# Reordered bit moves, block transposes and block loads in an attention-plus-MLP kernel

## The chip, the cores and the metric

The kernel runs on one core of one Trainium2 chip. The metric is the device time of one execution in microseconds (us), the median of several.

In the profile, TensorE's matmuls are PE and its weight loads PEld, VectorE is DVE, ScalarE is ACT, GpSimd is POOL, and SPq is the queue of SyncE, which issues most of the DMAs.

## The reference, cut to what matters

```python
q_bits = (einsum('bhsd,dk->bhsk', q, proj) > 0)       # 6 hash bits of each query, same for k
mask   = q_bucket[:, :, :, None] == k_bucket[:, :, None, :]
scores = where(mask, q @ k.T / sqrt(64), -1e9)        # batch 4, 8 heads, 768 x 768
attn   = softmax(scores) @ v
x = attn.transpose(0, 2, 1, 3).reshape(3072, 512)
out = silu(x @ w_in) @ w_out                          # 512 -> 2048 -> 512
```

The heads go in 16 pairs. The hash bits are put into spare rows of the q and k tiles, so that one matmul gives the score and the bucket's match; exp of it goes to the product with v. When the four pairs of a batch element are done, its MLP runs beside the attention of the next.

## The kernel before

The program is a list of 288 steps (w). At each step TensorE does one score matmul group, one attention step (av) and, from the ninth head on, a part of an MLP. Everything else is planned to a step, which sets the order in which instructions are given to their engines, and nothing more: an engine runs its own list as soon as each instruction's semaphores allow.

```python
    # pool tag "m": three PSUM buffers for h_ps, bp_ps (bit projections), tp_ps, and the MLP's outputs
    def mm1(ci, grp):
        hp = ps.tile([P, f, n], F32, tag="m", name="h_ps", bufs=3)
        ...                                        # TensorE: 4 matmuls of 128x512
        nc.scalar.activation(out=th, in_=hp, func=AF.Tanh, scale=0.5)
        after.append(lambda: nc.vector.scalar_tensor_tensor(   # g, at the next step; frees h_ps
            out=g[...], in0=th, scalar=1.0, in1=hp, op0=ALU.add, op1=ALU.mult))

    def bits_unit(pairs, i, par):                  # for pairs up to 7: two bit moves on VectorE
        for n in range(2):
            ...
            if n == 1 and par == 1:
                nc.vector.tensor_scalar(out=dst, in0=bits[pairs][r, :], ...)
            else:
                nc.vector.tensor_copy(out=dst, in_=bits[pairs][r, :])

    def block_unit(p, n):                          # L246
        nc.vector.transpose(out=dst, in_=qk_sb[p, "qk"[n]])

    t_first(1, 0, nc.vector.tensor_copy)           # start: second head's q out of PSUM
    ...
    for Q in range(2, NQUAD):                      # pairs 2Q and 2Q+1
        w0 = (Q - 1) * QST                         # QST = 36 steps
        for i in range(4 if Q > 2 else 0):
            w1 = w0 + (5, 9, 11, 14)[i]
            plan(w1, lambda Q=Q, i=i: block_unit(2 * Q + i // 2, i % 2))
            ...
        plan(w0 + 20, lambda Q=Q: proj_unit(2 * Q, 2 * Q + 1))
        for i in range(4):
            plan(w0 + 20,
                 lambda Q=Q, i=i: bits_unit((2 * Q, 2 * Q + 1), i // 2, i % 2))
        for i in range(2):
            ...
            for j in range(2):
                plan(w0 + 18 + 9 * i + 2 * j, lambda p=2 * Q + i, j=j: v_unit(p, (j,)))   # GpSimd
            if Q + 1 < NQUAD:
                plan(w0 + (20 if Q == 3 else 8) + i, lambda p=2 * Q + 2 + i: load_blocks(p))
    # x_unit(p), a transposing DMA on SyncE's queue, is planned at 2*NU*(p+1) + 9, that is 99 for p = 4
```

## Time and profile before

| | before |
|---|---|
| time, median of 3 (range) | 307.0 us (306.68 to 307.44) |
| the profiled execution | 308.2 us, span of the core 306.4 us |
| TensorE busy | 299.8 us, 98% of the span |
| TensorE's waits for a PSUM buffer that g frees | 2.4 us in two places |
| VectorE, ScalarE, GpSimd busy | 59%, 69%, 42% |

The lines themselves are in the prediction below. In the lines by time, the columns are start in us, length in us, engine, line of the kernel, operation, output<-input, shape, count; brackets at the end give how long the engine sat idle before the instruction and what ended it.

### The profile page before, as it was taken

The page shows a single profiled execution, that of the slowest core. Times are in us where ns is not written, and L with a number is a line of the kernel's source. Part 1 is how long each engine was busy: PE and PEld are TensorE (multiplying, and loading weights), DVE is VectorE, ACT ScalarE, POOL GpSimd, SP SyncE. Part 2 cuts the span into 40 slices and gives each one's busy share as a digit, 9 for nine tenths or more (in the row PEclk, how much of TensorE's full clock was granted, in tenths as well). Part 3 has the DMA queues.
Part 4 walks back from the last instruction along what each step waited for, and adds up shares of the span by engine and source line. Part 5 has one row for each costly group of instructions (what it writes and reads, how often), then busy time and mean ns, then how long its engine had stood idle before and what let it go on. Part 6 is the DMA issues. An engine that isn't in the chain of part 4 may idle for free.

```text
span 306.4 us, 7166 instructions
## 1 busy us (share of the span) xinstructions
PE 299.8 (98%) x2710; PEld 174.8 (57%) x2710; DVE 181.8 (59%) x342; ACT 210.2 (69%) x391; POOL 128.9 (42%) x203
## 2 busy tenths in 40 slices
PE   8999999988999999999999999999999999999996
PEld 3675855544666555545565665545566664446653
DVE  5797977789559534854597325864453342664332
ACT  5887989987777686878876666778877731543200
POOL 7589999368514842765138431675111100000000
PEclk9999999999999999999999999999999999999999
DMA  7999797999939825774048434111022013001112
GB/s 201 243 263 208 139 134 115 184 247 169 167 91 174 153 65 158 125 135 127 9 92 131 89 64 148 52 41 33 2 60 62 0 37 94 34 2 68 36 60 76
DMA packets 102786, 32.87 MB, mean 107 GB/s; under 512 B 90656, under 2 KB 99808, under 8 KB 102752
## 3 DMA queue, kind: packets, MB, share of 16 engines
q1 hardware_dynamic: 98368, 28.22, 42.8%
q0 software_dynamic: 4224, 4.19, 9.2%
q8 instruction: 21, 0.34, 0.5%
q14 instruction: 13, 0.11, 0.1%
q10 hardware_dynamic: 160, 0.00, 0.0%
HBM read 27.27 MB, written 6.29 MB: 110 GB/s over the span
## 4 chain that ended last, share of the span: by engine, by line
PE 89%; DVE 4%; DMA 4%; ACT 1%; SPq 1%; issue 0%; POOL 0%; ACTq 0%; POOLq 0%
PE o_ps L455 26%; PE h_ps L423 24%; PE s_ps L333 18%; PE o_ps L365 12%; DMA k_blk<-in_k_dram 4%; PE bp_ps L279 3%; PE tp_ps L185 2%; DVE g L429 1%; PE o_ps L441 1%; PE warm_ps L125 1%; PE tp_ps L198 1%; DVE qka L310 1%; PE bp_ps L225 1%; ACT u L336 1%; SPq L92 1%; DVE qk L246 1%
## 5 line engine op out<-in xcount | busy, mean ns | idle before, releaser
L336 ACT ACTIVATE u<-s_ps 128x512 f16<-128x512 f32 x288 | 156.3, 605 | 40.3 <-PE s_ps L333 39.8
L429 DVE SCALAR_TENSOR_TENSOR g<-th,h_ps 128x512 f16<-128x512 f32 x96 | 65.1, 684 | 75.9 <-ACT th L427 75.9
L423 PE MATMUL h_ps<-xT,win 128*128 128x512 f16 (+1 forms) x512 | 97.4, 325 | 2.4 <-DVE g L429 2.4
L365 PEld LDWEIGHTS <-u 128*128 128x128 f16 x1152 | 67.5, 98 | 42.8 <-ACT u L336 11.2
L455 PE MATMUL o_ps<-wout,g 128*128 128x512 f16 x368 | 91.6, 379 | 0.0
L427 ACT ACTIVATE th<-h_ps 128x512 f32<-128x512 f32 x96 | 57.3, 597 | 39.2 <-PE h_ps L423 36.0
L365 PE MATMUL o_ps<-vv,u 128*128 128x65 f16 x1152 | 82.8, 194 | 0.2
L423 PEld LDWEIGHTS <-win 128*128 128x128 f16 x512 | 49.9, 98 | 34.3 <-issue 3.0
L385 POOL TENSOR_TENSOR x_pr<-osum,rec 128x384 f16<-128x384 f32 x23 | 19.0, 824 | 90.5 <-DVE rec L384 90.1
L455 PEld LDWEIGHTS <-g 128*128 128x128 f16 x368 | 35.8, 98 | 34.1
L333 PE MATMUL s_ps<-qkb 128*128 128x512 f16 x192 | 52.8, 326 | 0.0
L333 PE MATMUL s_ps<-qka 71*128 71x512 f16 x192 | 52.7, 327 | 0.1
L251 POOL TENSOR_SCALAR qka<-qk 64x1536 f16<-64x1536 f32 x15 | 21.9, 1462 | 13.4 <-DVE qk L246 8.3
L460 DVE TENSOR_SCALAR osb<-o_ps 128x512 f32<-128x512 f32 x23 | 15.8, 685 | 15.5 <-PE o_ps L455 15.5
L251 POOL TENSOR_SCALAR qkb<-qk 64x1536 f16<-64x1536 f32 x15 | 22.0, 1468 | 1.2
L262 POOL TENSOR_TENSOR vsa<-v_sb 128x192 f32<-128x192 f32 x32 | 19.5, 609 | 0.0
L260 POOL CAST vv<-v_sb 128x384 f16<-128x384 f32 x32 | 16.4, 514 | 0.9 <-DMA v_sb<-in_v_dram 0.5
L246 DVE STREAM_TRANSPOSE qk<-k_blk 128x768 f32<-128x768 f32 x10 | 15.7, 1575 | 1.4 <-DMA k_blk<-in_k_dram 1.4
L333 PEld LDWEIGHTS <-qka 71*128 71x128 f16 x192 | 15.4, 97 | 0.7 <-ACT qka L238 0.5
L246 DVE STREAM_TRANSPOSE qk<-q_blk 128x768 f32<-128x768 f32 x10 | 15.7, 1574 | 0.0
L333 PEld LDWEIGHTS <-qkb 128*128 128x128 f16 x192 | 15.4, 97 | 0.0
L379 DVE TENSOR_TENSOR osum<-o_ps,vsum 128x390 f32<-128x390 f32 x23 | 13.0, 565 | 2.3
(64 smaller groups left out, 165.3 us busy)
## 6 DMA issues: line engine op xcount, KB each, us to landing
out_dram<-osb SPq DMA_DIRECT2D x23, 256.0 KB
v_sb<-in_v_dram SPq DMA_DIRECT2D x15, 384.0 KB
q_blk<-in_q_dram SPq DMA_DIRECT2D x40, 96.0 KB
k_blk<-in_k_dram SPq DMA_DIRECT2D x40, 96.0 KB
win<-in_moe_w_in_dram POOLq DMA_DIRECT2D x4, 512.0 KB, 6.9
wout<-in_moe_w_out_dram POOLq DMA_DIRECT2D x4, 512.0 KB, 7.4
q_sb<-in_q_dram SPq DMA_DIRECT2D x5, 384.0 KB
k_sb<-in_k_dram SPq DMA_DIRECT2D x5, 384.0 KB
```

Source lines behind the costliest of these rows:

```text
L246: nc.vector.transpose(out=dst, in_=qk_sb[p, "qk"[n]])
L251: nc.gpsimd.tensor_scalar(out=dst[rows, :], in0=qk32[p][rows, :], scalar1=CS, scalar2=1.0, op0=ALU.mult, op1=ALU.mult)
L260: nc.gpsimd.tensor_copy(out=vv[:, :, 0:D], in_=src)
L262: nc.gpsimd.tensor_tensor(out=sa, in0=src[:, 0:3], in1=src[:, 3:6], op=ALU.add)
L333: nc.tensor.matmul(sp[:, o0 : o0 + n], t[rows, S + jt * P : S + (jt + 1) * P], t[rows, c0 : c0 + n], start=True, stop=True)
L336: nc.scalar.activation(out=u, in_=sp, func=AF.Exp, scale=ESC)
L365: nc.tensor.matmul(o_ps[h][:, c0 // P + i, :], u[:, o0 + i * P : o0 + (i + 1) * P], vv[:, jt, :], start=(not direct(h) and w % NU == 0 and ...
L385: (nc.vector if direct(h) else nc.gpsimd).tensor_tensor(out=x_pr[p][:, :, par * D : (par + 1) * D], in0=o[:, 0:NJ, 0:D], in1=rec[:, :, Non ...
L423: nc.tensor.matmul(hp[:, j, :], w_in16[:, dt, ft * P : (ft + 1) * P], xT[4 * b + dt][:, c0 : c0 + n], start=(dt == 0), stop=(dt == NDT - 1))
L427: nc.scalar.activation(out=th, in_=hp, func=AF.Tanh, scale=0.5)
L429: after.append(lambda: nc.vector.scalar_tensor_tensor(out=g[ci][:, grp * f : (grp + 1) * f, :], in0=th, scalar=1.0, in1=hp, op0=ALU.add, o ...
L455: nc.tensor.matmul(o2[tt], g[ci][:, ft, ct * P : (ct + 1) * P], w_out16[:, ft, :], start=(ft == 0), stop=(ft == NFT - 1))
```

## The change

Its intent is to keep VectorE's queue from being blocked around the projection of pairs 6 and 7: transposes and bit moves are spread out, and SyncE's loads for the next pairs make room. One copy at the start goes to ScalarE. The whole diff:

```diff
-    t_first(1, 0, nc.vector.tensor_copy)
+    t_first(1, 0, nc.scalar.copy)
@@
-            w1 = w0 + (5, 9, 11, 14)[i]
+            w1 = w0 + (5, 9, 12, 15)[i]
@@
         for i in range(4):
-            plan(w0 + 20,
+            plan(w0 + 20 + (i if Q < 4 else 0),
                  lambda Q=Q, i=i: bits_unit((2 * Q, 2 * Q + 1), i // 2, i % 2))
@@
-                plan(w0 + (20 if Q == 3 else 8) + i, lambda p=2 * Q + 2 + i: load_blocks(p))
+                plan(w0 + (28 if Q == 3 else 8) + i, lambda p=2 * Q + 2 + i: load_blocks(p))
```

## The prediction

> **What bounds the kernel now.** I read the page first, then the waits of TensorE, then TensorE and VectorE in order of time around TensorE's two real gaps, then the DMA queue of SyncE, then the start. From the page, busy shares and the chain that ended last:
>
> ```profile
> PE 299.8 (98%) x2710; PEld 174.8 (57%) x2710; DVE 181.8 (59%) x342; ACT 210.2 (69%) x391; POOL 128.9 (42%) x203
> ...
> PE 89%; DVE 4%; DMA 4%; ACT 1%; SPq 1%; issue 0%; POOL 0%; ACTq 0%; POOLq 0%
> ```
>
> TensorE is busy in 299.8 of 306.4 us and carries 89% of the chain. Nothing in the change removes a matmul, so only TensorE's idle time, or stages in which it is not really full, can be gained. The waits of TensorE show how much of it a rearrangement could reach:
>
> ```profile
> PE h_ps L423 <- DVE g L429: 2.4, 2, 1.4
> ```
>
> Two waits, 2.4 us together, both for a PSUM buffer of tag "m" (three buffers, shared by h_ps, the bit projections bp_ps and the output projections) that VectorE must free by computing g. Where they are, in TensorE's order of time:
>
> ```profile
> 66.85 1.02 PE L423 MATMUL h_ps<-xT,win 128*128 128x512 f16 x4 [1.03 <-DVE g L429]
> ...
> 76.14 1.02 PE L423 MATMUL h_ps<-xT,win 128*128 128x512 f16 x4 [1.38 <-DVE g L429]
> ...
> 77.34 1.03 PE L423 MATMUL h_ps<-xT,win 128*128 128x512 f16 x4
> ...
> 78.88 1.03 PE L423 MATMUL h_ps<-xT,win 128*128 128x512 f16 x4
> ```
>
> And VectorE in the same stretch:
>
> ```profile
> 64.71 1.57 DVE L246 STREAM_TRANSPOSE qk<-k_blk 128x768 f32<-128x768 f32 x1 [1.39 <-DMA k_blk<-in_k_dram]
> 66.12 1.27 DVE L429 SCALAR_TENSOR_TENSOR g<-th,h_ps 128x512 f16<-128x512 f32 x2
> ...
> 69.44 1.25 DVE L285 TENSOR_SCALAR bits<-bp_ps,sc 128x512 f16<-128x512 f32 x2
> 70.73 1.15 DVE L310 COPY qka<-bits 13x768 f16<-13x768 f16 x2
> 71.89 0.65 DVE L310 COPY qkb<-bits 13x768 f16<-13x768 f16 x1
> 72.55 0.41 DVE L307 TENSOR_SCALAR qkb<-bits,sc 13x768 f16<-13x768 f16 x1
> 72.97 1.08 DVE L310 COPY qka<-bits 13x768 f16<-13x768 f16 x2
> 74.06 0.64 DVE L310 COPY qkb<-bits 13x768 f16<-13x768 f16 x1
> 74.71 0.65 DVE L307 TENSOR_SCALAR qkb<-bits,sc 13x768 f16<-13x768 f16 x1
> 75.40 1.88 DVE L429 SCALAR_TENSOR_TENSOR g<-th,h_ps 128x512 f16<-128x512 f32 x3
> ```
>
> The first gap (1.03 us) is a DMA's: the k block of pair 7 landed late, its transpose held VectorE's queue, and two g's stood behind it. The second (1.38 us) is one of order: after the projection of pairs 6 and 7, VectorE makes eight bit moves in one go (70.73 to 75.36) and only then the three g's that free the buffers. The first tanh of these three was ready at 71.94 (ScalarE's record: start 71.34, 0.60 long).
>
> **What the Trainium skill says.** "Perfetto Trace Analysis", section "Optimization Strategy": find the gaps of the bounding engine, find the semaphore it waits on, and let that dependency start sooner. The trace agrees that such gaps exist, 2.4 us in all. The same page, "Identifying the Most-Contended Engine", warns that matmul busy time does not measure the distance to the roofline. Here, too: between 44 and 53 us TensorE counts as busy for 8.98 of 9.00 us while weight loads wait for ScalarE's exp, which runs back to back. "DMA: Bandwidth & Descriptors", section "Queues, rings and completion order": on one DMA engine descriptors of a ring start in order, and an engine alternates between rings by packet. The trace agrees: from 54 to 63 us it has 1470 packets of 1024 B of the weight queue and 1497 of 128 B of the block loads, one to one. The section "Issuing engines are not separate DMA queues" says the same of queues of different issuers.
>
> **The change, part by part.** I compared the order of instructions on each engine in both programs.
>
> *Block transposes, steps 11 and 14 to 12 and 15.* On VectorE and GpSimd every transpose and cast stands at the same place as before; only buffer numbers differ, for pairs 6 and 7 and for the later ones. Engines see nothing but their own order and semaphores, so this is worth 0.
>
> *Bit moves over four steps.* For pairs 4 and 5, one xT copy of 0.56 us moves ahead of the last two moves, in a stage (about 47 us) in which TensorE waits for ScalarE, not for this copy: 0. For pairs 6 and 7, one g moves ahead of the last copy and the last tensor_scalar. That g then starts at 74.05 instead of 75.40 and ends at about 74.75. TensorE ran out of allowed work at about 74.6 (its last score matmul started at 74.38 and such a one takes 0.22 in the chain), so the matmuls of 76.14 start at about 74.8: 1.34 us sooner. But the next buffer is no sooner than VectorE: 74.75 + 0.65 (copy) + 0.65 (tensor_scalar) + 0.63 (second g, a third of 1.88) = 76.68, while TensorE would want it at 74.8 + 0.86 + 0.12 + 0.22 = 76.0 (four matmuls, an attention step and a score in the chain). So 0.7 us come back as a new, smaller wait, and the matmuls of 77.34 start at about 76.7: 0.64 sooner. The third needs a buffer freed at about 77.3 and starts 1.54 later than the second (78.88 - 77.34), at 78.24: no wait. From there VectorE has slack (idle from 79 us on) and TensorE stays 0.64 us ahead to the end. Value: **-0.64 us**.
>
> *Block loads of pairs 8 and 9 behind x of pair 4.* In SyncE's queue the transposing DMA of xT now comes before the sixteen block loads:
>
> ```profile
> 53.30 3.71 SPq L102 DMA_DIRECT2D v_sb<-in_v_dram  x2
> 57.10 9.80 SPq L92 DMA_DIRECT2D q_blk<-in_q_dram  x4
> ...
> 82.29 1.28 SPq L400 DMA_TRANSPOSE xT<-x_pr  x1
> ...
> 90.70 1.57 DVE L246 STREAM_TRANSPOSE qk<-q_blk 128x768 f32<-128x768 f32 x1
> ```
>
> x of pair 4 was ready at 58.88 (GpSimd's x_pr: 58.06 + 0.82), so SyncE waits about 1.8 us at 57.1, issues xT by about 60.2, then the blocks. SyncE is held after that by the landing of earlier loads (each load waits for the eighth before it), so the sixteen loads end about where xT ended, 83.6 us instead of 82.2, and land at about 86 at the latest (the last one landed at 84.7 before). VectorE wants the first at 90.70 and the last at 98.64: 5 us or more to spare. The early xT gains nothing, since the second batch's matmuls come far later (step 155, past 120 us). Could the k block of pair 7 land sooner? It was issued by 53.2, ahead of the loads that are moved, in the same rings. What starved it is the weight queue (three loads in flight from 51.8 on), which the change leaves where it is. It landed at 64.69, the weights at 64.86. So the 1.03 us gap stays: 0.
>
> *One copy at the start to ScalarE* (the diff has it, the title doesn't). ScalarE's order there:
>
> ```profile
> 7.09 0.51 ACT L238 COPY qka<-bits 7x384 f16<-7x384 f16 x1 [0.16 <-DVE bits L228]
> 8.35 2.06 ACT L336 ACTIVATE u<-s_ps 128x512 f16<-128x512 f32 x4 [0.76 <-PE s_ps L333]
> ```
>
> It is idle for 0.76 us before the first exp, and such a copy took it 0.48 us at 4.22: it ends at about 8.1, before 8.35. VectorE ends its pair of copies 0.5 us sooner and GpSimd's casts start 0.3 us sooner, but the next projection comes on TensorE behind the first attention step, which waits for that exp (8.95). Value 0, at most 0.1 either way.
>
> Sum: 307.0 - 0.64 = **306.3 us**.
>
> **Rivals.**
> 1. *The k block of pair 7 lands sooner without the block loads behind it.* Then the 1.03 us gap goes as well: 305.3, or 304.6 if the second gap went whole too. For it: that is what would motivate the move, and SyncE was held in that stretch. Against it: ring order, and the one-to-one packets show that the weights set the pace. I give it one in six.
> 2. *The delayed loads become the bound.* A transpose at 90.7 or later waits for a block, a g stands behind it, and TensorE waits as at 66.85, about 1 us each: 307 to 309. Against it: 5 us to spare. One in twenty.
> 3. *The second gap closes further or less.* The bit moves took 0.36 to 0.68 us for the same shape, whatever GpSimd did beside them. With two at 0.4, the second g comes 0.5 us sooner: 305.9. If everything VectorE saved is taken back by vsum and osum, which follow, 306.8.
> 4. *ScalarE is late at the start*, by up to 0.5 us, in a stage that ScalarE bounds: 306.8.
>
> **Range and chances.** The runs before spread over 0.76 us (306.68 to 307.44), more than the expected gain, so the median itself is uncertain by some 0.3 us. 80% range: 305.3 (rival 1) to 307.1 (no gain, noise up). 2% would be 6.1 us, over twice all the idle time that TensorE spends on waits; a loss of 6 us would take several new waits. Chances: faster 0.01, within 2% 0.98, slower 0.01.
>
> **What would show it.** In the changed profile, near 75 us: a g between the bit moves, the wait of 1.38 us gone or under 0.3, a new one of 0.4 to 0.9 us before the next h_ps matmuls. Near 65: the wait for k_blk of 1.4 us and TensorE's gap of 1.0 us still there; if they are gone, rival 1 was right and my reading of the rings wrong. xT issued at about 59 us, no wait of a transpose for a DMA after 90 us, and the exps starting at about 8.35 as before. A gain over 1.5 us, or a loss, makes the prediction wrong.

## The result, and the profile after

| | before | after |
|---|---|---|
| median of 4 runs (range) | 306.84 us (306.62 to 307.44) | 306.21 us (305.85 to 306.49) |
| ratio, 95% interval | | 0.9976 (0.9957 to 0.9994) |
| profiled execution (span) | 308.2 us (306.4 us) | 305.85 us (304.1 us) |

A ratio is the mean time of one kernel's fast runs over that of the other's of the same rounds, so it is not quite the ratio of the medians quoted beside it. The time is 0.1 us from the forecast. But the spans of the two profiles differ by 2.3 us, far more than the 0.6 us of the timed runs, so the two profiles may not be read against each other without care. The page of the changed kernel, busy shares and the chain that ended last:

```profile
PE 299.6 (99%) x2710; PEld 174.9 (58%) x2710; DVE 180.7 (59%) x341; ACT 210.7 (69%) x392; POOL 129.2 (42%) x203
...
PE 95%; DVE 3%; ACT 1%; issue 0%; POOL 0%; ACTq 0%; POOLq 0%
```

The 4% of DMA is gone from the chain. TensorE's order of time in the changed kernel, the matmuls that answer to those at 76.14, 77.34 and 78.88 before, and the first output matmuls:

```profile
73.48 1.03 PE L423 MATMUL h_ps<-xT,win 128*128 128x512 f16 x4
...
74.93 1.02 PE L423 MATMUL h_ps<-xT,win 128*128 128x512 f16 x4
...
76.47 1.03 PE L423 MATMUL h_ps<-xT,win 128*128 128x512 f16 x4
...
77.67 1.03 PE L455 MATMUL o_ps<-wout,g 128*128 128x512 f16 x4
```

No bracket of a wait is left on any of them. The first starts when TensorE is ready for it. The second could have started at 74.69 (the last score matmul before it began at 74.47 and takes 0.22) and starts at 74.93: a wait of 0.24 us that is too small for the view to show it. VectorE in the same stretch:

```profile
63.26 1.55 DVE L246 STREAM_TRANSPOSE qk<-k_blk 128x768 f32<-128x768 f32 x1
...
68.17 1.26 DVE L285 TENSOR_SCALAR bits<-bp_ps,sc 128x512 f16<-128x512 f32 x2
69.47 0.96 DVE L310 COPY qka<-bits 13x768 f16<-13x768 f16 x2
70.44 0.65 DVE L310 COPY qkb<-bits 13x768 f16<-13x768 f16 x1
71.09 0.41 DVE L307 TENSOR_SCALAR qkb<-bits,sc 13x768 f16<-13x768 f16 x1
71.52 1.08 DVE L310 COPY qka<-bits 13x768 f16<-13x768 f16 x2
72.63 0.69 DVE L429 SCALAR_TENSOR_TENSOR g<-th,h_ps 128x512 f16<-128x512 f32 x1
73.35 0.38 DVE L310 COPY qkb<-bits 13x768 f16<-13x768 f16 x1
73.74 0.42 DVE L307 TENSOR_SCALAR qkb<-bits,sc 13x768 f16<-13x768 f16 x1
74.19 1.28 DVE L429 SCALAR_TENSOR_TENSOR g<-th,h_ps 128x512 f16<-128x512 f32 x2
```

Two things are to be seen. The g stands where it was forecast, ahead of the last two moves; but these two now take 0.38 and 0.42 us, where they took 0.64 and 0.65 before. And the transpose of the k block of pair 7 waits for no DMA. SyncE's queue:

```profile
51.85 1.09 SPq L102 DMA_DIRECT2D v_sb<-in_v_dram  x2
69.66 1.77 SPq L400 DMA_TRANSPOSE xT<-x_pr  x1
71.52 6.17 SPq L92 DMA_DIRECT2D q_blk<-in_q_dram  x4
...
86.36 2.63 SPq L92 DMA_DIRECT2D k_blk<-in_k_dram  x4
```

SyncE sat from about 53 to 69.66 us waiting for x of pair 4, and the block loads behind it were issued from 71.5 to 89.0 us, not from 57.1 to 82.2. ScalarE at the start:

```profile
7.15 0.51 ACT L238 COPY qka<-bits 7x384 f16<-7x384 f16 x1 [0.16 <-DVE bits L228]
7.68 0.48 ACT L201 COPY qk<-tp_ps 128x384 f32<-128x384 f32 x1
8.41 1.08 ACT L336 ACTIVATE u<-s_ps 128x512 f16<-128x512 f32 x2 [0.25 <-PE s_ps L333]
```

The copy fits into the idle time before the first exp and ends at 8.16.

**Cutting the profiles into stages.** To compare single profiles I cut each at six places that are the same work in every kernel, by their starts in TensorE's order: A the first score matmul, B the first h_ps matmul, C the projection of pairs 6 and 7, D the first output matmul, E the projection of pairs 8 and 9, F the end of the last instruction that counts as busy. The experiments below are in the table already, since it is what most of them are read from.

| kernel | A | A to B | B to C | C to D | D to E | E to F |
|---|---|---|---|---|---|---|
| before | 7.94 | 45.50 | **14.72** | **11.93** | 23.46 | 200.36 |
| transposes_only | 8.84 | 45.50 | 13.54 | 11.60 | 23.47 | 200.36 |
| loads_only | 8.09 | 45.50 | 13.52 | 11.59 | 23.46 | 200.36 |
| no_bits | 10.12 | 45.50 | 13.52 | 11.60 | 23.47 | 200.43 |
| bits_only | 7.97 | 45.49 | 13.52 | **10.62** | 23.46 | 200.36 |
| after | 8.00 | 45.50 | 13.54 | **10.64** | 23.47 | 200.42 |
| after_again | 7.68 | 45.51 | 13.54 | **10.61** | 23.46 | 200.43 |
| no_loads | 8.44 | 45.51 | 13.54 | **10.64** | 23.46 | 200.42 |
| bits_wide | 7.99 | 45.50 | 13.55 | **10.56** | 23.46 | 200.36 |
| v_late | 9.51 | 45.51 | 13.52 | **10.53** | 23.46 | 200.36 |
| weights_early | 7.93 | 45.50 | 13.53 | 11.58 | 23.46 | 200.35 |
| weights_early_loads | 8.19 | 45.51 | 13.53 | 11.58 | 23.47 | 200.36 |
| bits_v_late | 7.81 | 45.52 | 13.53 | **10.39** | 23.46 | 200.35 |
| bits_v_late_early | 8.77 | 45.51 | 13.54 | **10.39** | 23.46 | 200.36 |

C to D is the stage that the experiments are about. The others repeat to 0.03 us, with three exceptions. A moves by over 2 us from one execution to the next (in no_bits, for one, TensorE's weight load of the first k rows waited 0.75 us for them to land). It makes the spread of the profiled executions: the spans of transposes_only, loads_only and no_bits are 305.8, 305.0 and 307.1 us, and less A all three are 296.9 to 297.0. B to C is 13.5 us in every profile but the very first, that of the kernel before, where the late k block made it 14.7 and left C to D 0.3 us longer. And E to F has two values some 0.07 us apart, of which more below. The six sum to 2.5 us less than the span before and after alike (303.9 of 306.4, 301.6 of 304.1), so nothing outside them differs. So the 2.3 us between the two spans are 1.2 us of an accident in one profile, 0.3 us of its aftermath, and 1.0 us of the change (11.60 to 10.64), less 0.06 us each by which A and E to F are longer after it.

### The profile page after: what moved, and what is told of

It is laid out like the page before. It is cut to its first block, busy times and chain, and to the rows that moved or that the text cites. A ratio compares the mean times of both kernels' runs of the same rounds, so it can differ in the third digit from the quotient of the medians.

```text
span 304.1 us, 7165 instructions
## 1 busy us (share of the span) xinstructions
PE 299.6 (99%) x2710; PEld 174.9 (58%) x2710; DVE 180.7 (59%) x341; ACT 210.7 (69%) x392; POOL 129.2 (42%) x203
## 4 chain that ended last, share of the span: by engine, by line
PE 95%; DVE 3%; ACT 1%; issue 0%; POOL 0%; ACTq 0%; POOLq 0%
PE h_ps L423 26%; PE o_ps L455 26%; PE s_ps L333 20%; PE o_ps L365 13%; PE bp_ps L279 3%; PE tp_ps L185 2%; PE o_ps L441 1%; PE warm_ps L125 1%; DVE g L429 1%; DVE qka L310 1%; ACT u L336 1%; PE bp_ps L225 1%; PE tp_ps L198 1%; PE o_ps L356 0%; DVE bits L285 0%
```

## The experiments

Twelve kernels ran, in three calls of four; the kernels of a call shared eleven runs of the kernel before on their chip (medians 306.97, 306.79 and 306.61 us). All were correct.

### The four parts one by one

**transposes_only**, which is the null:

```diff
-            w1 = w0 + (5, 9, 11, 14)[i]
+            w1 = w0 + (5, 9, 12, 15)[i]
```

> Only the block transposes are moved (steps 11 and 14 to 12 and 15). Every engine's order of instructions is the same as before but for buffer numbers, so this is a null: all theories say ratio 1.000, within 0.001, and its spread is the noise for the others. It is also a second profile of the program before: my theory says that the late k block of pair 7 (VectorE waits 1.4 us for it, TensorE 1.0 us) was an accident of that one profiled execution (308.2 us against a median of 306.8), so it should be absent or different here, while the gap of TensorE before the h_ps matmuls behind the eight bit moves (1.4 us) should be there again, 0.6 to 1.4 us. The rival (the block loads of pairs 8 and 9 delay that k block in every execution) says that the wait for k_blk of about 1.4 us is there again.

Measured: 306.83 us, ratio 1.000 (0.9984 to 1.0016). This is the noise of the method: an interval of 0.16% either way. The program is the kernel before, engine by engine, and its profile is the more usual one. TensorE:

```profile
75.54 1.02 PE L423 MATMUL h_ps<-xT,win 128*128 128x512 f16 x4 [1.05 <-DVE g L429]
```

The gap behind the bit moves is there (1.05 us), the gap and the wait for the k block of pair 7 are not. The late block was an accident, as expected, and not what this kernel usually does.

**bits_only** and **no_bits**, the bit moves alone, and everything but them:

```diff
# bits_only, against before
-            plan(w0 + 20,
+            plan(w0 + 20 + (i if Q < 4 else 0),
# no_bits, against after: the same line put back
```

> Only the bit moves are spread over four steps. My theory, that all of the gain is the one g that goes ahead of the last two bit moves: ratio 0.9976 (0.997 to 0.9985), -0.6 to -0.8 us, the gap of TensorE near 75 us down from 1.4 to under 0.7 us. The rival, that the moved loads give the gain: 1.000.

> The changed kernel with the bit moves back in one step; the loads, the transposes and the copy at the start stay changed. My theory: ratio 1.000 within 0.001, the gap of TensorE behind the eight bit moves is back (0.6 to 1.4 us). The rival, that loads or the start give the gain: 0.9976.

Measured: bits_only 305.73 us, ratio 0.9961 (0.9946 to 0.9976), more gain than the range that I had expected, C to D 10.62 us and no wait of h_ps for g that the view shows. no_bits 307.48 us, ratio 1.0021 (0.9999 to 1.0042), C to D 11.60 us and the gap back at 1.04 us. The bit moves carry the whole gain; without them the rest of the change gains nothing. The 0.2% by which no_bits looks slower is more than the 0.1% that I had allowed for, but 1.000 lies at the edge of its interval, and its profile shows no wait that the kernel before lacks, except for the start (A at 10.12).

**loads_only**, the block loads alone:

```diff
-                plan(w0 + (20 if Q == 3 else 8) + i, lambda p=2 * Q + 2 + i: load_blocks(p))
+                plan(w0 + (28 if Q == 3 else 8) + i, lambda p=2 * Q + 2 + i: load_blocks(p))
```

> Only the block loads of pairs 8 and 9 are moved behind x of pair 4. My theory: ratio 1.000 within 0.001; the loads are issued some 12 us later than before and no transpose waits for them. The rival, that the loads were in the way of the k block of pair 7: ratio 0.997 to 0.998 and no wait for k_blk in the profile.

Measured: 307.28 us, ratio 1.0006 (0.999 to 1.0022), and the stages of the null. No transpose waits for the later loads.

**after_again** and **no_loads**, the changed kernel with and without its moved loads, because the first runs of the change (0.9976) and bits_only (0.9961) left room for a cost of the loads:

```diff
# no_loads, against after
-                plan(w0 + (28 if Q == 3 else 8) + i, lambda p=2 * Q + 2 + i: load_blocks(p))
+                plan(w0 + (20 if Q == 3 else 8) + i, lambda p=2 * Q + 2 + i: load_blocks(p))
```

> The changed kernel again, now beside the next kernel on one chip. The first four profiles cut into stages say that the bit moves shorten the stretch from the projection of pairs 6 and 7 to the first output matmuls from 11.60 to 10.62 us and that everything else is equal, so: ratio 0.9968 (0.996 to 0.998), the stretch 10.6 us. If the moved loads take something back (the change gave 0.9976 in its first runs, the bit moves alone 0.9961), it is again nearer to 0.9976 than the kernel without them.

> The changed kernel with the block loads back in their old place (bit moves, transposes and the copy at the start stay changed). My theory: the same as the changed kernel within 0.001, 0.9968. The rival (the later loads cost something): 0.9961 or less, and more than 0.001 below the changed kernel. In the profile the loads of pairs 8 and 9 are issued from 54 us on, not from 70 us.

Measured: 305.85 us, ratio 0.9964 (0.9951 to 0.9978) with the loads moved, and 306.17 us, 0.9968 (0.9951 to 0.9984) without. They are equal, as are their stages. The change is worth 0.36% here and 0.24% in its first runs, with overlapping intervals; the stages say 1.0 us, 0.32%.

### Why 1.0 us and not 0.64: what the bit moves run beside

In transposes_only, VectorE's last two moves and the g's behind them:

```profile
73.45 0.65 DVE L310 COPY qkb<-bits 13x768 f16<-13x768 f16 x1
74.11 0.66 DVE L307 TENSOR_SCALAR qkb<-bits,sc 13x768 f16<-13x768 f16 x1
74.80 1.88 DVE L429 SCALAR_TENSOR_TENSOR g<-th,h_ps 128x512 f16<-128x512 f32 x3
```

and GpSimd in the same kernel at the same time:

```profile
73.29 0.52 POOL L260 CAST vv<-v_sb 128x384 f16<-128x384 f32 x1
73.77 0.78 POOL L262 TENSOR_TENSOR vsa<-v_sb 128x192 f32<-128x192 f32 x1
74.63 0.32 POOL L264 TENSOR_TENSOR vsb<-vsa 128x64 f32<-128x64 f32 x1
```

The slow moves run beside a cast and a large add of one head's v. In the changed kernel, GpSimd:

```profile
72.44 0.52 POOL L260 CAST vv<-v_sb 128x384 f16<-128x384 f32 x1
72.93 0.58 POOL L262 TENSOR_TENSOR vsa<-v_sb 128x192 f32<-128x192 f32 x1
73.59 0.32 POOL L264 TENSOR_TENSOR vsb<-vsa 128x64 f32<-128x64 f32 x1
73.99 0.36 POOL L265 TENSOR_TENSOR vs<-vsb,vsa 128x64 f16<-128x64 f32 x1
```

Now the g (72.63 to 73.32) lies beside the cast and the large add, and the two moves (from 73.35) beside the small adds, but for the last 0.16 us of the large one. The Trainium skill, "SBUF — State Buffer", section "Who interferes with whom", says that VectorE and GpSimd share one pair of SBUF ports, that copies and tensor_scalars in certain modes want it, and that the second to ask for it is blocked. To test that on this kernel, **v_late** keeps all eight moves in one go and takes GpSimd's work away from beside them:

```diff
-                plan(w0 + 18 + 9 * i + 2 * j, lambda p=2 * Q + i, j=j: v_unit(p, (j,)))
+                plan(w0 + (30 if Q == 3 else 18) + 9 * i + 2 * j, lambda p=2 * Q + i, j=j: v_unit(p, (j,)))
```

> The program before, bit moves in one step, but GpSimd's work on v of pairs 6 and 7 comes twelve steps later. Theory: the last two bit moves take 0.65 us each because they run beside GpSimd's cast and add of v, and 0.4 us each where they run beside its small adds; that is why the change gained 1.0 us and not 0.64. Then the moves at the end are 0.4 us each here, most of the eight are shorter, and TensorE's gap shrinks from 1.05 to 0.5 us or less: ratio 0.998 (0.9965 to 0.999). The rival (the moves are faster in the changed kernel because a g comes ahead of them): the moves stay at 0.65 us, the gap at 1.05 us, ratio 1.000.

Measured: 305.90 us, ratio 0.9967 (0.995 to 0.9984). VectorE and then GpSimd in v_late:

```profile
73.57 0.35 DVE L310 COPY qkb<-bits 13x768 f16<-13x768 f16 x1
73.94 0.42 DVE L307 TENSOR_SCALAR qkb<-bits,sc 13x768 f16<-13x768 f16 x1
74.38 1.88 DVE L429 SCALAR_TENSOR_TENSOR g<-th,h_ps 128x512 f16<-128x512 f32 x3
```

```profile
71.08 0.80 POOL L172 DMA_DIRECT2D wout<-in_moe_w_out_dram  x1
77.39 0.82 POOL L385 TENSOR_TENSOR x_pr<-osum,rec 128x384 f16<-128x384 f32 x1 [5.51 <-DVE rec L384]
```

The last two moves take 0.35 and 0.42 us with GpSimd idle and no g between them. The eight together take 3.28 us, against 4.36 in transposes_only and 3.86 in the changed kernel. The first g starts 5.84 us after the projection (74.38 - 68.54) instead of 6.92 (74.80 - 67.88), and the view shows no wait of TensorE for g any more. It is not quite gone:

```profile
74.77 0.38 PE L333 MATMUL s_ps<-qkb 128*128 128x512 f16 x1
75.12 1.02 PE L423 MATMUL h_ps<-xT,win 128*128 128x512 f16 x4
```

The score takes 0.22 us in the chain, so the h_ps matmuls could have started at 74.99 and waited 0.13 us, where I had expected up to 0.5. So the rival (moves are quicker because a g comes ahead of them) falls: what they run beside sets their length. Taking GpSimd away gains as much (C to D 10.53) as the change of order.

The traces say more than these two moves. Over all 14 profiles, 324 moves of this shape (13x768) began while an arithmetic instruction of GpSimd was running, and every one ended 0.20 to 0.30 us after that instruction did. A move beside GpSimd is not a slower move but one that can't end before its neighbour: the 324 took from 0.35 to 1.59 us, the longest beside GpSimd's scaling casts of q and k, of 1.46 us each; the 20 moves with GpSimd wholly idle took 0.35 to 0.42. That is the blocking of which the page tells. GpSimd's issue of a DMA can hold a move too: those that began during its issues of w_out loads, some 0.8 us each, took 0.68 to 0.69 us in 13 of 14 profiles, in v_late too.

**bits_wide** puts the four groups of moves two steps apart, and so all three g's ahead of the last two moves:

```diff
-            plan(w0 + 20,
+            plan(w0 + 20 + (2 * i if Q == 3 else 0),
```

> The program before with the four groups of bit moves of pairs 6 and 7 two steps apart, so that all three g's are ahead of the last two moves. If order on VectorE is all there is to it, the rest of TensorE's gap (0.24 us in the changed kernel) goes too: the stretch from the projection to the first output matmuls 10.4 us, ratio 0.9960 (0.995 to 0.997), no wait of h_ps for g. If the three g's were the limit themselves, 10.6 us as with one step apart.

Measured: 305.94 us, ratio 0.9974 (0.9954 to 0.9995), C to D 10.56, not 10.4. The two h_ps matmuls do start without a wait, but the output matmul behind them starts at 77.60 though the score ahead of it began at 77.22 and takes 0.22: a new wait of 0.16 us. In VectorE's order, the two moves that now stand between the g's lie beside GpSimd's cast and large add:

```profile
71.52 0.69 DVE L429 SCALAR_TENSOR_TENSOR g<-th,h_ps 128x512 f16<-128x512 f32 x1
72.23 1.59 DVE L310 COPY qka<-bits 13x768 f16<-13x768 f16 x2
73.86 1.28 DVE L429 SCALAR_TENSOR_TENSOR g<-th,h_ps 128x512 f16<-128x512 f32 x2
```

They take 1.59 us for two, instead of 1.08 in the changed kernel. Order alone wasn't all there was to it; by these spans, what was won in order was partly lost beside GpSimd, though no run takes GpSimd's work away with this order.

### Was the late k block the loads' doing?

The accident happened once in fourteen profiles, so it had to be made to happen. **weights_early** issues two weight loads some 7 us sooner, where they meet the block loads of pairs 6 and 7; **weights_early_loads** has the change's load order as well, so that nothing is queued behind the k block:

```diff
# weights_early, against before; weights_early_loads has the diff of loads_only as well
-        plan((24, 40, 68, 74)[i], lambda i=i: load_w_in(i))
+        plan((24, 40, 52, 53)[i], lambda i=i: load_w_in(i))
```

> The program before, but two weight loads (w_in, third and fourth quarter) are issued at steps 52 and 53 instead of 68 and 74, some 7 us sooner, so that they run beside the block loads of pairs 6 and 7 in every execution. Theory: the weight queue, taking turns packet by packet, starves those loads; the k block of pair 7 lands at 64 us or later, its transpose waits for it on VectorE, and TensorE loses 1 us or more as in the profile of before: the stretch from the first h matmuls to the projection of pairs 6 and 7 is 14.5 us or more instead of 13.5, ratio 1.003 to 1.02. If the late block was not the weights' doing: 13.5 us, 1.000.

> As weights_early, and the block loads of pairs 8 and 9 moved behind x of pair 4, so that nothing of them is in flight while the k block of pair 7 lands. My theory (order within the rings): the k block is as late as in weights_early, within 0.5 us, and so is the stretch. The rival (loads queued behind it delay it, which would have been a reason for the change): it lands 1 us or more sooner than in weights_early, and the ratio is nearer to 1 by 0.003 or more.

Measured: 306.73 us, ratio 1.0004 (0.998 to 1.0029), and 306.77 us, 0.9996 (0.9977 to 1.0015). The expected stall did not come: B to C is 13.53 in both. I had the landing too late. Counted in the packets of the traces, the last block packet of pairs 6 and 7 came 8.36 us after B (at 61.8 us) in weights_early, and VectorE wanted the block at 63.19. (These loads have 768 packets of 128 bytes each, so their last is number 12288.) In the seven profiles from transposes_only to no_loads in the table, with the usual weight order, it came -0.1 to 3.0 us after B, and in the slow profile of before 10.84 us after it. So the weights do make the block late, by 5 us and more, and still not late enough to cost anything here.

Nor does the pair decide the other question. The last block packet came 8.36 us after B in both, but in weights_early SyncE issued the first load of pair 8 only from 61.58 to 62.15 us, when that packet was as good as there (61.79). So no load of pairs 8 and 9 stood behind the k block in either kernel; the pair shows that the weights are enough to make it late.

What the other question needs is in the slow profile of before, where the first load of pair 8 was issued at 57.10 to 58.32 us, with the k block still under way. In the three microseconds before (from 55) the block queue moved 173, 176 and 234 packets, in the four after (from 58) 175, 177, 169 and 180, against 1181 in the one from 52 us, before the weights came. And when number 12288 was through, by 64.3 us, no other block packet moved until the wait for the k block had ended (64.69). So the load behind neither overtook the k block nor changed its pace. This is one load in one execution; with more of them queued it is not tested. That TensorE loses 1 us when the block comes that late is shown only by this profile too; why this one execution fell behind by itself stays open.

### Versions meant to be better

**bits_v_late** joins the spread moves (for pairs 6 and 7) with v_late; **bits_v_late_early** also puts the block loads of pairs 6 and 7 ahead of x of pair 1, so that they are done before the weights begin:

```diff
# both
-            plan(w0 + 20,
+            plan(w0 + 20 + (i if Q == 3 else 0),
-                plan(w0 + 18 + 9 * i + 2 * j, lambda p=2 * Q + i, j=j: v_unit(p, (j,)))
+                plan(w0 + (30 if Q == 3 else 18) + 9 * i + 2 * j, lambda p=2 * Q + i, j=j: v_unit(p, (j,)))
# bits_v_late_early alone
-                plan(w0 + (20 if Q == 3 else 8) + i, lambda p=2 * Q + 2 + i: load_blocks(p))
+                plan(w0 + (20 if Q == 3 else 5 if Q == 2 else 8) + i, lambda p=2 * Q + 2 + i: load_blocks(p))
```

> A version meant to be the best: the bit moves of pairs 6 and 7 over four steps, and GpSimd's work on v of these pairs twelve steps later. TensorE's own work between the projection and the first output matmuls is about 10.4 us, so no more than 10.4 is left of the stretch (10.62 in the changed kernel, 10.53 in v_late): ratio 0.996 (0.995 to 0.9975), not to be told from the changed kernel by timing, but with no gap of TensorE in that stretch of the profile.

> As bits_v_late, and the block loads of pairs 6 and 7 ahead of x of pair 1 in SyncE's queue, so that they are done before the weight loads of 52 us begin. Typical executions do not wait for them, so the median is that of bits_v_late within 0.001; the k block of pair 7 should land at 50 us or earlier. If the earlier loads get in the way of something (weights, x of pair 1), the first h matmuls come later than 45.5 us after the first score matmul and the ratio is worse.

Measured: bits_v_late 305.55 us, ratio 0.9958 (0.9941 to 0.9974), C to D 10.39 as forecast. The projection and the first output matmuls in its profile:

```profile
66.87 1.50 PE L279 MATMUL bp_ps<-qk,pw 128*32 128x512 f32 x16
77.26 1.03 PE L455 MATMUL o_ps<-wout,g 128*128 128x512 f16 x4
```

TensorE has no gap left between the two, as forecast. This kernel has the lowest median of all that were tried and takes 0.25 us less from C to D than the changed kernel; by timing the two cannot be told apart (0.9958 and 0.9964). They were run at other times. bits_v_late_early: 306.04 us, ratio 0.9973 (0.9956 to 0.9989). The last packet of the blocks came 3.9 us before B (at 50.3 us), a little later than the 50 us or earlier that I expected, and no stage is worse than in bits_v_late but A, which scatters by itself. The ratio is 0.0015 above that of bits_v_late, where I had expected 0.001 at most, but inside both intervals, if only just. It is a safeguard against the accident; since that accident did not recur, no run shows that it helps, and by timing it is not better.

## Why the prediction was right, point by point

**The bit moves.** The mechanism was right and its size off. The g came ahead of the last two moves, the wait of 1.38 us vanished, and a smaller one took its place on the second matmuls. The term that was mis-sized is "74.75 + 0.65 (copy) + 0.65 (tensor_scalar)": they took 0.38 and 0.42, because moving the g also moved the moves to another neighbour on GpSimd (v_late). The new wait is 0.24 us, not 0.7, and the gain 0.98 us by stages (11.60 to 10.62), not 0.64. The third rival had this outcome, but with the words "0.36 to 0.68 us for the same shape, whatever GpSimd did beside them", and those are refuted: it is what GpSimd did beside them. It was a misreading even of the trace that I had: three moves of this shape at 18.55, 30.52 and 32.12 us took 1.53 to 1.59 us there, each beside GpSimd's casts of 1.46 us.

**The start of the gap.** The 1.38 us that I took as given were those of one execution; in transposes_only, loads_only and no_bits the gap was 1.04 to 1.05 us. From where TensorE ran out of work to its next matmuls, I forecast that 0.9 of 1.54 us would be left (0.2 before the first matmuls, 0.7 before the second); measured, 0.24 of 1.21 are (75.54 less 74.33 in transposes_only). So two errors, too much left and too long a gap to begin with, partly cancelled.

**The other gap (1.03 us, the k block of pair 7).** "So the 1.03 us gap stays: 0" was wrong as a statement about the profile, where it is gone, and right about the change: it is also gone in kernels whose loads were not moved (transposes_only, bits_only, no_loads). I had read an accident of a slow execution (308.2 us against 306.68 to 307.44) as the rule. The reading of the rings, that a load queued behind the block does not delay it, fits the packets of the slow profile, the only one in which such a load was queued in time; the weights_early pair did not test it. My first rival, that the gain comes from the moved loads, is refuted by loads_only (1.0006): in the usual execution the k block is not late at all.

**The block loads of pairs 8 and 9.** "x of pair 4 was ready at 58.88" was a misreading: the x_pr at 58.06 is that of the pair's first head. The second head's came at 70.26 to 71.08. So SyncE waited some 17 us, not 1.8, and the last blocks were issued up to 89.0 us, not 83.6. The conclusion survived by luck: the last block packet came at about 91.3 us in the changed kernel, and VectorE wanted that block at 96.23, some 5 us later. That the queue stands while its head waits fits the Trainium skill ("DMA: Bandwidth & Descriptors", section "Anatomy of one DMA — SWDGE (gpsimd) path": a semaphore wait happens on the issuing sequencer before dispatch), and the trace shows it, with nothing issued on SyncE from 52.94 to 69.66 us; I had only misjudged how long.

**The transposes and the start.** Both are 0 as worked out: transposes_only 1.000, and A to B 45.49 to 45.52 us with the copy on either engine. The bit moves of pairs 4 and 5, which the change spreads as well, also lie in A to B, and so are worth 0, as forecast. The four kernels with that copy on ScalarE (after, after_again, no_loads, no_bits) have some 0.07 us more from E to F than the others. In all four it arises at one place, an exp of ScalarE 9.2 us after E that starts 0.1 us later; I have no explanation for it.

**The sum.** 306.3 us against 306.21 measured is closer than the terms deserve: the first runs of the change came out at 0.63 us, the second ones at 0.94 (306.79 to 305.85), and the stages say 0.98. The noise that I allowed for, 0.3 us on a median, was right.

## What to carry to other kernels

When a queue of small VectorE moves holds up the instruction that frees a PSUM buffer, put that instruction first, and look at what GpSimd does at the same time: here, a move that began beside one of its instructions ended only after it, and took almost twice as long beside the large casts and adds of v, and removing that neighbour was worth as much as the new order. Planned positions that leave every engine's own order as it was were worth nothing here (transposes_only, 1.000), and this could be seen before any run. Before a wait in a profile is taken as the kernel's habit, compare the profiled execution's time with the timed runs, and cut the profiles into stages of equal work: most stages repeated to 0.03 us here where whole executions scattered by 2 us.

## What the Trainium skill lacked or had wrong

- "SBUF — State Buffer" ("Who interferes with whom") has the rule that VectorE and GpSimd block each other on a shared port pair, and the runs agree (324 moves, none of which ended before its neighbour on GpSimd). It gives no number for small f16 moves: a 13x768 f16 copy took 0.35 us with GpSimd idle and 0.65 us beside its cast and add of v, while g (one input in PSUM) had a median of 0.69 us with GpSimd idle and with GpSimd busy in the changed kernel. Nor does it say that a DMA issue of GpSimd can hold up VectorE: moves that began during its w_out issues took 0.68 to 0.69 us in 13 of 14 profiles.
- "DMA: Bandwidth & Descriptors" ("Queues, rings and completion order") says that an engine alternates between rings by packet. It does not draw the consequence for rings with packets of unequal size: with 1470 packets of 1024 B against 1497 of 128 B in 9 us, the ring of small packets got an eighth of the bytes of the other. In weights_early, where the weights met the block loads in this way, the last block packet came 5 us and more later (8.36 us after B, against -0.1 to 3.0).
- No page that I used says how far one profiled execution may lie from the timed ones: the first score matmul came at 7.7 to 10.1 us in fourteen profiles of nearly the same program, and one of them had a stall of 1.2 us that none of the others had.
